# Logits summed by heads in all row blocks but the last, early loads for the last convolution, and a new written order

## The chip, the cores and the metric

The kernel runs on one core of one Trainium2 chip. The metric is the time of one execution on the device in microseconds (us). Of the kernel before there are three timed runs: 394.6, 395.1 and 396.57 us, median 395.1. The core has five engines with a queue each: TensorE (PE in the profile; its weight loads are PEld), VectorE (DVE), ScalarE (ACT), GpSimd (POOL) and SyncE (SP), which here issues nearly all DMAs. An engine takes its instructions strictly in the order of its queue.

## The reference

Four layers on x of 2048 rows and 512 columns in bfloat16: attention, convolution, attention, convolution, each on the layer-normalized x and added to x. The weights of the two attentions are the same, and those of the two convolutions too.

```python
def _A_ref(x, wqkv, wo):                      # 32 heads of 16, window 8, dilation 2
    qkv = (x @ wqkv).reshape(B, S, 3, H, Dh).transpose(2, 0, 3, 1, 4)
    q, k, v = qkv[0], qkv[1], qkv[2]
    idx = pos[:, None] - arange(8)[None, :] * 2   # masked where negative
    logits = einsum("bhsd,bhswd->bhsw", q, k[idx]) * Dh ** -0.5
    o = einsum("bhsw,bhswd->bhsd", softmax(logits), v[idx])
    return o.transpose(0, 2, 1, 3).reshape(B, S, D) @ wo

def _B_ref(u, A, B, C, log_dt, Dskip):        # a long convolution per column
    P = exp((exp(log_dt) * A)[:, :, None] * arange(L))
    K = einsum("dn,dnl,dn->dl", C, P, exp(log_dt) * B).real
    y = irfft(rfft(u, 2 * L) * rfft(K, 2 * L))[:L]
    return y + u * Dskip

x = x + _A_ref(layernorm(x)); x = x + _B_ref(layernorm(x))
x = x + _A_ref(layernorm(x)); x = x + _B_ref(layernorm(x))
```

## The kernel before

**Stages.** Six stages follow each other. Generation (`k_gen`, 0 to 107.9 us of the profile) builds the convolution kernel K from powers of the complex exponentials, and beside it normalizes x, turns it, makes the keys and queries of the first attention and its first three products. First attention (`LayerA.core` with CORE0, to 185.1). First convolution (`FftB.run` with ORDER0, to about 236.6), which also transforms K. The front of the second attention (ORDERF, to about 262): the end of the first convolution, normalization, transposes, keys. Second attention (`core` with CORE1, to 347.7). Second convolution (ORDER1, to 389.1), after which the last stores land.

**The order is written out by hand.** In a region of `tc.manual_schedule(engines=...)` each named engine issues its instructions as they are emitted. The strings ORDERK, CORE0, ORDER0, ORDERF, CORE1 and ORDER1 give the order of emission, one letter or word a step. Before, each stage has a region of its own, and where the instructions of one region fall among those of the next or among what stands between regions (loads, pools) is the scheduler's affair. The tile framework adds the waits between engines.

**An attention.** Rows lie as position p*16 + a, so a row block a of 128 rows holds every sixteenth; four of them are one block q (q = 0 to 3). The queries, keys and values of a block are projections on TensorE (`qproj1` L219, `front_k` L277, `v_proj` L395), each four matmuls into PSUM and a copy out by ScalarE (or DVE). The letters in the two CORE strings:

- m: a product of a block's queries with the eight shifted keys of one quarter ft of the columns (DVE, L342), into one of two buffers `prod`; l: its sum over the columns of a head on TensorE into the block's logits L (L350 or L354); x: their maximum (DVE, L414); e, r, n: exponentials and normalization (TensorE and ScalarE, L430 to L453).
- A block with q < NCOL sums by heads: eight matmuls with the 32 head indicators as weights stream the products, and the logits stand with the heads on the partitions; they are turned after the softmax (T, `turn` L455: eight transposes and a ScalarE copy). Another block sums by rows: 32 matmuls with the products as weights and eight columns of indicators. Before, NCOL is (2, 2).
- P: the products of one row block's attention with its eight shifted values (DVE, L472); S or V: their sum and transposition on TensorE by 64-row halves (S, L497) or whole (V, L487), with a ScalarE copy; O: the output projection, with the statistics for the next normalization; a and f: the normalization of one row block on DVE or ScalarE (L197, L195); b, d, t: its statistics.
- After the eighth and the sixteenth value projection SP copies rows of v_ext into its first part (L403, L404); the products P of even and of odd row blocks need the first and the second of these copies.
- Other letters are events of the stage: in CORE0 the tables of the inverse transform (c, 2 to 5), loads of K (1, 6), its rearrangement into k_perm (A to H, by the engine in KROWS), and w, the load of the matrix w2 in 32 DMAs (L596). In CORE1 the events 0 to 3 are what the front leaves over: keys of block 3 (P3), queries (Q0), and copies of shifted keys (x, e; `front_ext`).

**A convolution.** K and U (first transform step of K and of u), k and u (second step, with w2), m (the product of both spectra, DVE, L857), y or Y (first inverse step), and z, w, v (second inverse step, added to x). The letter A or D behind a step names the engine that copies the result out of PSUM. u goes through three buffers `ub`. In the first convolution the spectrum of K is stored to DRAM (`kf_dram`); the second reads it back into a ring of seven slots and three spare ones, three DMAs a slot (`kf_load`, L847, L849). The ring and the table g2 are allocated and asked for when the second convolution is opened (`open_mid`, L768), which the scheduler may place among the earlier stages' DMAs.

In generation the letters are: s, i, b (squares, products and copies of powers), M (one table of powers, DVE), T, U (the levels of another, DVE), p (their product on TensorE) and x (copied out), y and z (normalization, by the engines in ENGK), X (the first attention's first three products) and Z (their sums).

```python
    with tc.manual_schedule(engines=MAN_ALL):
        C = k_gen(...)
```

## Time and profile before

| what | value |
| --- | --- |
| median of three runs | 395.1 us (394.6 to 396.57) |
| profiled execution: span, its own time | 393.9 us |
| VectorE busy | 372.8 us, 95% |
| ScalarE busy | 331.1 us, 84% |
| TensorE busy | 324.1 us, 82% |
| GpSimd busy | 65.5 us, 17% |
| TensorE clock granted | 0.999 |
| DMA traffic | 54.18 MB |

The profile is of one execution; the page gives its span, from the first to the last instruction, as the only time of that execution. In a table by stage, a row has the stretch in us, its length, then busy time and number of instructions for each engine, the granted clock, the mean busy share of the 16 DMA engines and GB/s. In a list in order of time a row has start, length, engine, line of the kernel, operation, the tile written and those read, their shapes, how many instructions are merged in the row, and, in brackets, how long the engine idled before it and what ended that. Neighbouring instructions of one engine can overlap by some 0.1 us, so the distance of two starts is a better price than a length. In the groups, behind the shape and the number of instructions stand their busy time in us, the mean length in ns, and the idle time before them.

### The profile page before, as it was taken

The page shows a single profiled execution, that of the slowest core. Times are in us where ns is not written, and L with a number is a line of the kernel's source. Part 1 is how long each engine was busy: PE and PEld are TensorE (multiplying, and loading weights), DVE is VectorE, ACT ScalarE, POOL GpSimd, SP SyncE. Part 2 cuts the span into 40 slices and gives each one's busy share as a digit, 9 for nine tenths or more (in the row PEclk, how much of TensorE's full clock was granted, in tenths as well). Part 3 has the DMA queues.
Part 4 walks back from the last instruction along what each step waited for, and adds up shares of the span by engine and source line. Part 5 has one row for each costly group of instructions (what it writes and reads, how often), then busy time and mean ns, then how long its engine had stood idle before and what let it go on. Part 6 is the DMA issues. An engine that isn't in the chain of part 4 may idle for free.

```text
span 393.9 us, 14769 instructions
## 1 busy us (share of the span) xinstructions
PE 324.1 (82%) x6451; PEld 231.5 (59%) x6499; DVE 372.8 (95%) x449; ACT 331.1 (84%) x568; POOL 65.5 (17%) x97
## 2 busy tenths in 40 slices
PE   3000258999999999999998899999999999998894
PEld 2000116756734676766887888543456676677894
DVE  6999999999989999999999989979999999989984
ACT  7999999997558799899999998574666779889992
POOL 9402960000280000010731201100000020000000
PEclk9999999999999999999999999999999999999999
DMA  7953810414027556277678634820253057604525
GB/s 209 396 155 50 83 53 3 106 28 108 9 66 198 128 168 176 61 228 235 215 265 300 216 110 110 300 62 2 73 141 96 3 170 222 195 13 155 171 68 152
DMA packets 68303, 54.18 MB, mean 138 GB/s; under 512 B 33545, under 2 KB 58670, under 8 KB 67982
## 3 DMA queue, kind: packets, MB, share of 16 engines
q1 hardware_dynamic: 66566, 48.70, 42.7%
q0 software_dynamic: 1664, 4.52, 3.1%
q8 instruction: 51, 0.84, 0.9%
q14 instruction: 14, 0.11, 0.1%
q10 hardware_dynamic: 8, 0.00, 0.0%
HBM read 30.15 MB, written 13.24 MB: 110 GB/s over the span
## 4 chain that ended last, share of the span: by engine, by line
PE 49%; DVE 21%; ACT 19%; issue 5%; DMA 2%; SPq 2%; POOL 1%; DVEq 0%; ACTq 0%; POOLq 0%
PE pq L398 7%; PE po L497 5%; PE pq L508 4%; PE pq L223 4%; PE pk L1277 3%; DVE A_t L1119 3%; ACT ub L869 3%; DVE B_t L1119 3%; PE L L354 3%; PE pp L282 3%; ACT a1s L800 3%; PE pp L1215 2%; DVE t L857 2%; SPq L596 2%; PE L L350 2%
## 5 line engine op out<-in xcount | busy, mean ns | idle before, releaser
L472 DVE TENSOR_TENSOR pav<-attn,v_ext 128x4096 bf16<-128x4096 bf16 (+1 forms) x34 | 72.3, 2160 | 0.3 <-DMA v_ext<-v_ext 0.3
L342 DVE TENSOR_TENSOR prod<-qT,kT_ext 128x4096 bf16<-128x4096 bf16 x29 | 65.6, 2288 | 3.0 <-PE L L350 2.1
L1119 DVE TENSOR_TENSOR A_t<-A_t,pow_t 128x1024 bf16<-128x1024 bf16 (+4 forms) x46 | 38.2, 873 | 0.2
L1205 PE MATMUL pt<-ident,x_blk 128*128 128x128 bf16 x64 | 6.0, 241 | 39.4 <-ACT x_blk L195 39.4
L508 PE MATMUL pq<-wop,oT 128*128 128x512 bf16 x121 | 31.5, 379 | 2.4 <-issue 1.9
L497 PEld LDWEIGHTS <-pav 64*128 64x128 bf16 x1728 | 26.9, 95 | 9.9 <-DVE pav L472 3.3
L869 ACT CAST ub<-pb 128x1024 bf16<-128x1024 f32 x32 | 32.6, 1110 | 0.0
L1215 PE MATMUL pp<-xnT,kT_ext 128*128 128x512 bf16 x88 | 25.5, 413 | 7.3 <-ACT xnT L1208 4.3
L818 PE MATMUL pb<-a1s,w_sb 128*128 128x64 bf16 x768 | 27.4, 193 | 3.8 <-ACT ub L869 1.4
L398 PE MATMUL pq<-wv,xnT 128*128 128x512 bf16 x123 | 30.0, 379 | 0.5 <-ACT kgs L1285 0.3
L497 PE MATMUL po<-ident,pav 64*128 64x64 bf16 x1728 | 29.9, 190 | 0.6 <-ACT oT L499 0.2
L400 ACT CAST v_ext<-pq 128x512 bf16<-128x512 f32 x32 | 18.7, 586 | 13.5 <-PE pq L398 11.1
L800 ACT CAST a1s<-pb 128x1024 bf16<-128x1024 f32 x29 | 28.5, 1063 | 1.2 <-PE pb L811 1.2
L1205 PEld LDWEIGHTS <-x_blk 128*128 128x128 bf16 x64 | 4.6, 107 | 41.3 <-ACT x_blk L195 40.2
L818 PEld LDWEIGHTS <-w_sb 128*128 128x128 bf16 x768 | 25.1, 98 | 6.0 <-issue 4.0
L178 POOL TENSOR_TENSOR ln_rstd<-ln_rstd,ln_mh 128x4 f32<-128x4 f32 x2 | 4.0, 1995 | 120.1 <-DVE ln_rstd L177 66.9
L1277 PEld LDWEIGHTS <-A_t 128*64 128x64 bf16 (+1 forms) x512 | 21.7, 103 | 3.8 <-DVE A_t L1119 0.2
L800 DVE CAST a1s<-pb 128x1024 bf16<-128x1024 f32 x19 | 22.5, 1220 | 1.4 <-PE pb L811 1.0
L1277 PE MATMUL pk<-B_t,A_t 128*64 128x84 bf16 (+1 forms) x512 | 23.5, 201 | 0.2
L223 PE MATMUL pq<-xnT,kT_ext 128*128 128x512 bf16 x85 | 22.6, 379 | 0.9 <-issue 0.5
L225 ACT CAST qT<-pq 128x512 bf16<-128x512 f32 x24 | 14.0, 585 | 9.8 <-PE pq L223 9.5
L398 PEld LDWEIGHTS <-xnT 128*128 128x128 bf16 x128 | 11.9, 97 | 15.3 <-issue 2.4
(264 smaller groups left out, 919.9 us busy)
## 6 DMA issues: line engine op xcount, KB each, us to landing
w_sb<-w_dram SPq DMA_DIRECT2D x64, 128.0 KB, 3.0
w_dram<-xnT SPq DMA_DIRECT2D x1, 4096.0 KB
kf_ring<-kf_dram SPq DMA_DIRECT2D x13, 256.0 KB, 3.8
kf_ring<-kf_dram SPq DMA_DIRECT2D x26, 128.0 KB, 3.6
v_ext<-v_ext SPq DMA_DIRECT2D x4, 784.0 KB, 6.1
x_blk<-in_A_x_dram SPq DMA_DIRECT2D x4, 512.0 KB, 4.7
kT_ext<-in_A_wqkv_dram SPq DMA_DIRECT2D x4, 512.0 KB, 9.2
x_sb<-in_A_x_dram SPq DMA_DIRECT2D x4, 512.0 KB, 6.3
```

The lines of the kernel that those rows point to most:

```text
L223: nc.tensor.matmul(pq[:], lhsT=self.wqk[:, dt, ft * P:(ft + 1) * P], rhs=self.xnT[:, dt, q * 512:(q + 1) * 512], start=(dt == 0), stop=(dt ...
L342: nc.vector.tensor_tensor(pr, self.qT[q][:, ft].unsqueeze(1).to_broadcast([P, W, 4, P]), kap, ALU.mult)
L398: nc.tensor.matmul(pp[:], lhsT=xnT[:, dt, a * P:(a + 1) * P], rhs=wv[:, dt, :], start=(dt == 0), stop=(dt == NDT - 1))
L472: nc.vector.tensor_tensor(pv[:, i], attn[:, n % 4].unsqueeze(2).to_broadcast([P, W, DH // parts, H]), vap, ALU.mult)
L497: nc.tensor.matmul(po[:, h, 0, i * nt + ft, :], lhsT=pvf[rows, i, w, ft * P:(ft + 1) * P], rhs=ident[rows, rows], start=(w == 0 and ft + i ...
L508: nc.tensor.matmul(pw[:], lhsT=oT[:, ftp, :], rhs=self.wo[:, ftp, :], start=False, stop=(ftp == NDT - 1))
L800: (self.nc.scalar.copy if eng == "act" else self.nc.vector.tensor_copy)(dst, src)
L818: nc.tensor.matmul(p2[:, j, :], lhsT=self.w2[:, ec * EC + j, :], rhs=a1s[:, ec * EC + j, :], start=True, stop=True)
L869: nc.scalar.copy(ub[:], p2)
L1119: return lambda: nc.vector.tensor_tensor(*args)
L1215: nc.tensor.matmul(pps[kind, b, ft][:], lhsT=la.wqk[:, dt, c:c + P], rhs=la.xnT[:, dt, b * 512:(b + 1) * 512], start=(dt == 0), stop=(dt = ...
L1277: nc.tensor.matmul(o, lhsT=lhs, rhs=Bt[:, ri, c * CH + ql].rearrange("p b g -> p (b g)"), start=(not half and j % 4 == 0 and ri == 0), sto ...
```

## The change

- NCOL becomes (4, 3): all four blocks of the first attention and the first three of the second sum their logits by heads; block 3 of the second stays by rows.
- The whole program is one region in which DVE, ScalarE, TensorE and SP issue in the order of emission; GpSimd is ordered in generation alone, as before.
- In the second attention g2 and the seven ring slots get tiles of their own on the other side of the memory, allocated before `core`, and are asked for by the events 0 to 3 of CORE1, behind the front's remaining steps; the convolution starts with these seven slots filled and asks for three more. In the first convolution g2 is asked for by the word g of ORDER0.
- The w2 load is cut into four parts (W) of eight DMAs.
- The front's thirteen remaining steps become events of their own (RKEYS), each with its engine (RROWS).
- All six order strings are others. In ENGK two normalizations (y, z) go from DVE to ScalarE; in KROWS two parts of k_perm go from ScalarE to DVE.

```diff
-sbiCCiCisCGiCbiMsaibsCbMiibMcMsTibMGicGMMbasMGiGibTMTMbsGGTabbiTTiaTsicGTbbacTiTibcGsTMTGiaGaMlM
...
-kUTzkzUkTxkTKttkKkUkUkpKekekxKUUpkkKqxpKUqUUxUkUoEUUkpQkUKkpxUUoxpUXpxXKopxxZXZZ
+iCsCaibCiCbMsiGMisbisCMiibbCMsaiibcMTMMbcisGibbscbGMTibTiTsMbTbTciibTMasTaGcTGaGMaGaiiMMTGGGMlaG
...
+kkkKkTkUlkKzUzTUTqzUzpUpUUUtKxpeUtUqUExUQepkkUUxxkUKUpEpokxXkUKkoKkkxpKpZXoXxXZZ
 """
 ORDER0 = """
-KD KA KA KA KA KD KD KA KA KD kA KD KA KD KA kA kD UA KD UA UD UA UA UD UA UD
-kA KD kA kD u kD u m u kA kD UA UA m u kD UA kD m UA UA u m kD UA m
-u u UD UA m u kA u m m kA kD kA m yD u m u YA m u YA yD u u m
-m YA u m u m w000A m YA yA YD YA yA yD yA w010D yA
+g KD KA KA KA KA KD KD KA KA KD KA kD KA KD KA KD kA UA UD KA UD kA UD UA kD UA UD UA kA kD u kD u m
+m u u kA kD u kD UA UA m UA m u UD u kD UA UA m m m u UA kA kD UA kA m kD kA u yD u u m YD u m m m
+YA yA u u u m u YA w000A YA m m m yD YA YA yA yD yA w010D yA
 """
 ORDERF = """
-yD h00 h01 yA YA v101A v100A v110A v111A h10 z12A a0 p0 v113A h11 a1 p1 z02A S z03A n0D T0 n1G E00D
-v103D E01A P03 H2 a2 T1 P01 E10D p2 E11D Q00 n2G H3 P00 a3 P02 P11 P12 p3 T2 E21D E20D P10 P13
-P22 P20 n3D T3 E31A P23 P21 E30D x1
+yD h01 yA YA v100A v101A h00 v110A v111A h10 a0 v103D p0 n0D v113A h11 z03A S a1 z12A T0 E01D E00A
+p1 z02A n1G P02 H2 Q00 P01 T1 a2 E10A p2 P03 E11D P10 P00 n2G H3 P12 a3 T2 E20A p3 P13 E21D n3D P23
+P11 P21 T3 E30D P20 E31D x1D P22
 """
 ORDER1 = """
...
-YA m m m w001A w000D yA yA w011D YA w010D yA yD yA yD yA v102D v101A v112D v111A v113D v103D v100A v110D
...
+v112D v110D v113D v103D v101A v111A
 """
 CORE0 = """
-vmvvvvqlvmxvlmemvvrclvnlmqTlqmxmvvelvvvvcmlqcPlSPrqOmncml1VTxPPqeSmr2lqP4OlSOSm5PqOP3S7lmOSnlPOx
-VPeOPSPrOSnPO6SObbP9SwOP8SPdBHOVaOPfSEdObatSaCaAfataGDFO
+mmvvvvlcvvmvllxemvmqrlmcnvlcxqTqvlcvvmmevvvvPqlr1qlPmnql4VTmmqO3lxSPq62lOS57mPlePSmOrSlPnOSPO8xT
+SPbeOSrOPSnOPSTOPP9SbdOSPfdOPSOSaaPPfOFSfAOSfabWWWWODtGtCEHfB
 """
 CORE1 = """
-0m1l2ml3mqvvmvllqvmqvxqelmlvmmvvqrlnqlmTvmxPPvlvvqvvqvmlmvqlqelmSrqnxmPSPqTOSOSlePOlPmrSOSnmOOPl
-bSlPSPwOxdfPVaePOSraPOnVabPOSPdOSOPSbPOSfaOftSdafaaftO
+DACBFGEJIvHmKmllLN0123qmvqvmlvqmllvvmxvvqlqmemlqrlmnvqTvxmevllvPqvvvmvmqPlrlnmxqqTmSleqSmlPrOSOP
+PmSnOSPPTOlblSOSPOxSedPOOrPSbnSPfdPOSWWWWfPOSOPSfPOSafOSbPdOafaStatafOf
 """
-NCOL = (2, 2)
-ENGK = dict(b="AAAAAAAAAAAAAAAAA", y="AAAAAAAAAADA", z="DAAA", e="AAAAAAAA", K="AAAAAAAAAAAAAAAA", Q="AAAAAAAA", x="AAAAAAAAAAAAAAAA")
+NCOL = (4, 3)
+ENGK = dict(b="AAAAAAAAAAAAAAAAA", y="AAAAAAAAAAAA", z="AAAA", e="AAAAAAAA", K="AAAAAAAAAAAAAAAA", Q="AAAAAAAA", x="AAAAAAAAAAAAAAAA")
 STATD = (3,)
-KROWS = "DADAADDD"
+RKEYS = "ABCDEFGHIJKLN"
+RROWS = "AADDAADAAADDA"
+KROWS = "DDDDDADD"
...
+    def load_w2(self, w2_dram, part):
+        if part == 0:
+            w2 = self.keep.tile([P, NDT * (2 * D + (NA + 14) * P)], BF16, name="w2_sb", tag="slot")
...
+        for c in range(8 * part, 8 * part + 8):
             self.nc.sync.dma_start(self.w2[:, c * 4:(c + 1) * 4, :], w2_dram[:, c * 4:(c + 1) * 4, :])
...
+def kf_read(nc, kc, kf_dram, n):
+    g, ec = divmod(n, NEC)
+    nc.sync.dma_start(kc[0::2], kf_dram[g, ec])
+    for r in range(2):
+        nc.sync.dma_start(kc[1::2, r], kf_dram[g, ec, :, 1 - r])
...
     def open_mid(self):
         tc, nc, t = self.tc, self.nc, self.tag
-        nc.sync.dma_start(self.g2[:], self.g2_dram[:])
         if t:
-            for n in (4, 3):
-                kr = self.c_mid.enter_context(tc.tile_pool(name=f"b{t}_kf{n}", bufs=1, reuse_waits="tile"))
-                kr = kr.tile([P, n, 2, DQG, EC], BF16, name=f"kf_ring{n}")
-                self.ring += [kr[:, i] for i in range(n)]
+            self.nkf = len(self.ring)
+            self.kf = dict(enumerate(self.ring))
             self.ring += self.extra
...
     nc = tc.nc
+    ctx.enter_context(tc.manual_schedule(engines=MAN))
...
-    with tc.manual_schedule(engines=MAN_ALL):
+    with tc.manual_schedule(engines={ET.Pool}):
         C = k_gen(tc, nc, lambda sp: build_a_consts(nc, cpool, sp, consts), ins, kd, la, x_v, lnst,
...
-        ev = {"w": lambda: la.load_w2(w2_dram),
-              "0": last(("P", 3, 0), ("P", 3, 1), ("x", 0), ("x", 2), ("P", 3, 2), ("Q", 0, 1), ("e", 0), ("Q", 0, 2)),
-              "1": last(("P", 3, 3), ("Q", 0, 3)), "2": last(("e", 1), ("e", 2)), "3": last(("e", 3))}
...
+    ring_ctx = ExitStack()
+    g2p = ring_ctx.enter_context(tc.tile_pool(name="b1_g2", bufs=1, side="right", reuse_waits="tile"))
+    g2 = g2p.tile([P, 2, 16, P], BF16, name="g2_sb")
+    ring = []
+    for n in (4, 3):
+        kr = ring_ctx.enter_context(tc.tile_pool(name=f"b1_kf{n}", bufs=1, side="right", reuse_waits="tile"))
...
+    ev = la.w2_loads(w2_dram)
+    ev |= {"0": lambda: nc.sync.dma_start(g2[:], g2_dram[:]), "1": lambda: ring_loads(0, 1), "2": lambda: ring_loads(2, 3),
+           "3": lambda: ring_loads(4, 5, 6)}
+    rest = (("P", 3, 0), ("P", 3, 1), ("x", 0), ("x", 2), ("P", 3, 2), ("Q", 0, 1), ("e", 0), ("Q", 0, 2),
+            ("P", 3, 3), ("Q", 0, 3), ("e", 1), ("e", 2), ("e", 3))
+    for c, e, (op, *ix) in zip(RKEYS, RROWS, rest):
+        ev[c] = lambda e=e, op=op, ix=ix: front[op](*ix, dict(A="act", D="dve")[e])
```

130 lines of the change are left out of this document (64 added, 66 removed).

## The prediction

> **What bounds the kernel now.** I read the page's busy shares first, then a table of busy time by stage, then the instructions in order of time at the joins of the stages, and last the groups by shape, for prices.
>
> ```profile
> span 393.9 us, 14769 instructions
> PE 324.1 (82%) x6451; PEld 231.5 (59%) x6499; DVE 372.8 (95%) x449; ACT 331.1 (84%) x568; POOL 65.5 (17%) x97
> ```
> ```profile
> core 0: us, PE busy (x) PEld busy (x) DVE busy (x) ACT busy (x) POOL busy (x), PEclk, DMA share, GB/s
> 0.00:107.90 107.90, 56.93 (x702) 38.68 (x712) 103.64 (x168) 96.33 (x178) 33.73 (x49) 1.00 0.43 109
> 107.90:185.10 77.20, 74.69 (x1496) 46.82 (x1513) 75.19 (x61) 66.00 (x129) 10.27 (x19) 1.00 0.55 155
> 185.10:236.60 51.50, 46.92 (x1440) 43.65 (x1435) 49.89 (x52) 51.13 (x58) 15.03 (x25) 1.00 0.63 222
> 236.60:262.00 25.40, 24.77 (x231) 16.98 (x231) 22.45 (x69) 18.34 (x35) 3.50 (x4) 1.00 0.59 183
> 262.00:347.70 85.70, 83.18 (x1552) 49.98 (x1569) 83.75 (x70) 62.28 (x130) 2.94 (x1) 1.00 0.36 105
> 347.70:389.10 41.40, 37.59 (x1045) 35.37 (x1044) 37.91 (x36) 37.04 (x42) 0.00 (x0) 1.00 0.39 117
> ```
>
> The stages are: kernel generation, first attention, first convolution, the front of the second attention, second attention, second convolution. VectorE (DVE) idles 21.1 us in all, and 4.3 of that lies in generation and 4.8 behind the last instruction. In both attentions DVE (75.19 of 77.20, 83.75 of 85.70) and TensorE (74.69, 83.18) are both nearly full; the first convolution is bound by ScalarE (51.13 of 51.50); the front by TensorE (24.77 of 25.40). So DVE work that is removed counts in the first, second and fifth stage alone, TensorE work in the fifth, and ScalarE work only where it delays the third.
>
> **The engine sums.** Shape by shape:
>
> ```profile
> L197 DVE TENSOR_SCALAR xnT<-x_sb,ln_rstd,ln_nb 128x512 bf16<-128x512 bf16 x16 | 6.3, 415 | 0.1
> L195 ACT ACTIVATE xnT<-x_sb,ln_nb,ln_rstd 128x512 bf16<-128x512 bf16 x8 | 6.4, 814 | 0.0
> L1459 DVE COPY k_perm<-k_rl 128x1024 bf16<-128x1024 bf16 x5 | 2.0, 421 | 0.0
> L1459 ACT COPY k_perm<-k_rl 128x1024 bf16<-128x1024 bf16 x3 | 3.1, 1044 | 0.2 <-DMA w_sb<-w_dram 0.2
> L273 DVE COPY xnT<-pt 128x1024 bf16<-128x1024 bf16 x6 | 3.9, 678 | 1.2 <-PE pt L271 1.2
> L295 DVE COPY kT_ext<-kT_ext 128x508 bf16<-128x508 bf16 x5 | 1.4, 290 | 0.2 <-ACT kT_ext L285 0.2
> L461 ACT COPY attn<-L 128x1024 bf16<-128x1024 bf16 x4 | 4.1, 1017 | 0.5 <-PE L L459 0.5
> L800 DVE CAST a1s<-pb 128x1024 bf16<-128x1024 f32 x19 | 22.5, 1220 | 1.4 <-PE pb L811 1.0
> ```
>
> DVE: two normalizations of generation go to ScalarE (y and z of ENGK), -2 x 0.415 = -0.83. In CORE0 three more do ("a" 6 to 3, "f" 2 to 5), -1.25, and two parts of k_perm come back (KROWS), +0.84. In ORDER0 K has two DVE evacuations fewer, k one and U one more: 4 x 1.22, sum 0. In ORDERF one E goes to ScalarE, -0.68, in a stage that TensorE bounds, so it is worth nothing. In the second attention one kT copy (-0.29) and two normalizations (-0.83) go. On DVE's path that is -0.83 - 0.41 - 1.12 = -2.4; six small instructions that run on the heels of others cost some 0.08 less than their duration, so I take **-2.0** (bounds -1.5 and -2.4).
>
> ScalarE takes what DVE gives (7 x 0.814, less 2 x 1.044, and about 1.6 for the E and the kT copy) and three copies of turned attention, 3 x 1.017: some 8 us. In the attentions its cover is 11.2 us of idle time in the first (77.20 - 66.00) and 23.4 in the second. If that cover were gone, in the first it would delay the ScalarE-bound convolution: see rival C.
>
> TensorE: prices by starts of neighbours, 119.01 to 119.56 (0.55) for a sum by heads, 126.63 to 127.44 (0.81) by rows, 118.47 to 119.01 (0.54) for eight 128-column matmuls, which is also what turning a block takes. The two last rows are from the chain of waits.
>
> ```profile
> 118.47 0.61 PE L441 MATMUL pq<-ex,ident 128*128 128x128 bf16 x8
> 119.01 0.61 PE L350 MATMUL L<-prod,ind 128*32 128x512 bf16 x8
> 119.56 0.39 PE L398 MATMUL pq<-wv,xnT 128*128 128x512 bf16 x1
> 126.63 0.94 PE L354 MATMUL L<-ind,prod 128*128 128x8 bf16 x32
> 127.44 3.61 PE L398 MATMUL pq<-wv,xnT 128*128 128x512 bf16 x15
> 138.48 1.89 PE po L487 x32
> 153.30 1.11 PE po L497 x64
> ```
>
> Blocks 2 and 3 of the first layer and 2 of the second change form: 12 sums, -12 x 0.26 = -3.1, and three turns, +1.6. Four rows of the attention output that were summed whole (V, 1.8) are summed by halves (S, 1.1): -2.8. In all -4.3, of which 4 x 0.26 - 0.54 + 2 x 0.7 = 1.9 lies in the second attention. The mask matmuls (0.2) stay. [...]
>
> **The joins.** The first attention starts late:
>
> ```profile
> 101.31 6.69 DVE L342 TENSOR_TENSOR A_pr<-qT,kT_ext 128x4096 bf16<-128x4096 bf16 x3
> 107.91 0.29 DVE L295 COPY kT_ext<-kT_ext 128x508 bf16<-128x508 bf16 x1
> 109.78 4.50 DVE L342 TENSOR_TENSOR prod<-qT,kT_ext 128x4096 bf16<-128x4096 bf16 x2 [1.57 <-PE L L350]
> ```
>
> Its first product waits 1.57 us until the third of generation's products is summed, because TensorE has value projections in between. With one region for the program TensorE keeps the written order, the sums (Z Z) first and "mm vvvv" after them: the third sum follows its product by 0.55, less the 0.29 copy that runs meanwhile, plus a hand-over of 0.1. The wait becomes 0.4: **-1.2** (bounds 0 and -1.57). TensorE then starts its projections 1.3 us later; the order has room for that: by adding up each queue from the start of the stage (0.86 a projection, 0.55 or 0.81 a sum, 2.2 a product), the last sum of block 2 has 26.9 us of TensorE work up to its end and DVE asks for it after 28.7 us of its own work, where before the pair is 29.4 against 28.7. The closest pair is the second sum of block 2, 23.2 against 24.3.
>
> The front: TensorE does as many projections behind the last transposes as before.
>
> ```profile
> 257.35 1.06 PE L271 MATMUL pt<-ident,xn 128*128 128x128 bf16 x16
> 258.24 4.26 PE L282 MATMUL pp<-xnT,kT_ext 128*128 128x512 bf16 x19
> 261.98 2.29 DVE L342 TENSOR_TENSOR prod<-qT,kT_ext 128x4096 bf16<-128x4096 bf16 x1
> ```
>
> Two projections of block 2 and one of block 3 (0.86 each), an evacuation and a copy come before the first product in both orders, so 3.74 us behind the transposes: 0. In the second attention DVE now idles 1.95. In the new order the third product must wait for the first sum, which has eight projections ahead of it: 258.24 + 10 x 0.86 + 0.55 = 267.4 against 261.98 + 2 x 2.2 + 0.4 = 266.8, a wait of 0.6. The next pairs come out within 0.2 of each other (the sum of product (0,3) ends 14.2 us of TensorE work after 259.97, at 274.2; product (1,1), which needs its buffer, is due at 267.4 + 3 x 2.2 = 274.0), and in the second half TensorE is ahead by 2, having 1.9 us less. I leave 1.25 of the 1.95: **-0.7** (bounds -1.4 and +0.7).
>
> Generation's order: DVE asks for the ninth power (for product step 17) 31.7 us into its own work, and ScalarE has it after 33.4; the largest such lead before was 1.3 us and made no wait. **+0.4** (bounds 0 and +1). First convolution: equal sums, ScalarE full, so nothing to gain; products now come two and three together with three ub buffers, **0** (bounds -0.3 and +1.5). Second convolution: as many instructions on each engine as before, **0** (bounds -0.5 and +0.5).
>
> The DMAs: by its name the change asks for the ring early. Before, SP does so already:
>
> ```profile
> 246.13 0.51 SPq L847 DMA_DIRECT2D kf_ring<-kf_dram  x1
> 246.69 1.24 SPq L849 DMA_DIRECT2D kf_ring<-kf_dram  x2
> 255.75 0.59 SPq L849 DMA_DIRECT2D kf_ring<-kf_dram  x1
> 281.46 0.67 SPq L403 DMA_DIRECT2D v_ext<-v_ext  x1
> 283.18 2.04 SPq L849 DMA_DIRECT2D kf_ring<-kf_dram  x1
> v_ext<-v_ext SPq DMA_DIRECT2D x4, 784.0 KB, 6.1
> ```
>
> Five ring slots are asked for from 246 on and the rest from 283, and the second convolution shows no wait for them: so this part does little here, 0. The w2 loads in four parts and the g2 load stay in SP's order.
>
> Sum: -2.0 - 1.2 - 0.7 + 0.4 = -3.5 on the profiled 393.9, which lies 1.2 below the median of the three runs (395.1): taken off that, **391.6**. The runs differ by 2 us, so 0.5% (2.0 us) is about what can be told from no change.
>
> **The rivals.** B, the waits go too: with TensorE relieved, all of DVE's idle time in the front and the second attention (2.95 + 1.95, of which 0.7 is counted) but some 1 us vanishes: 391.6 - 3.2 = 388.4. For it: TensorE is what these waits name (L271, L350). Against: the front keeps its TensorE work.
>
> C, handed back: ScalarE's added work in the first attention (3 x 0.81 - 2 x 1.04 + 2 x 1.02 = 2.4) arrives at the convolution that it bounds, and all gained before it (0.8 + 0.4 + 1.2 - 0.4 = 2.0) is lost: 393.6. Against: ScalarE idles 11 us there, though most of it before 130.
>
> D, slower: SP's queue in the second attention. The written order puts g2 and seven ring slots (22 DMAs, 1.9 us a slot by the rows from 246.13 on, 13.7 in all) ahead of the copies of v_ext, for which the first output product waits. Their room is that of the front's xn, last read by the transposes at 258.24; SP is then at v_ext by 272, and the copies have 1.6 to issue and 6.1 to land. The product comes near 287, so the ring must begin by 266. If its room is only free with something later, every us beyond 266 is a us: held until 272.5, the time is 391.6 + 6.5 = 398.1.
>
> [...]
>
> **How the numbers follow.** Forecast 0.45 (its own range 390 to 393), B 0.15, C 0.2, D 0.15, E 0.05. Faster by over 0.5% (under 393.1): forecast and B, 0.6; within: C and E, 0.25; slower (over 397.1): D, 0.15. The range goes from B (388.4 less 0.4 for the runs' lower spread, 388.0) to a D that is 3 us late with the upper spread of 1.5, 396.2.
>
> **What would show it.** Right: the first product of the first attention follows the last of generation with under 0.7 us of idle; DVE near 370 busy; the first convolution starts near 182.5 and takes as long as now; the second attention shortens by 1.5 to 2. Wrong: a DVE wait for v_ext's DMA near 287 (D), a ScalarE that enters the first convolution behind DVE (C), waits for ub in it, or generation ending after 108.

## The result and the profile after

The changed kernel takes 390.43 us (median, 390.08 to 391.12), the kernel before 395.34 in runs beside it: ratio 0.9868 with a 95% interval of [0.9844, 0.9893], 4.9 us faster, by the interval 1.1 to 1.6%. The profiled execution took 390.13, its span is 388.4, 5.5 under the span of before. From the page: the span, the busy shares, and, from its part on the DMA queues, the queue that brings instructions (packets, MB, share of the engines).

```profile
span 388.4 us, 14497 instructions
...
PE 319.6 (82%) x6312; PEld 219.9 (57%) x6361; DVE 369.8 (95%) x442; ACT 336.1 (87%) x578; POOL 68.2 (18%) x97
...
q8 instruction: 49, 0.80, 0.8%
```

The table of busy time by stage:

```profile
core 0: us, PE busy (x) PEld busy (x) DVE busy (x) ACT busy (x) POOL busy (x), PEclk, DMA share, GB/s
0.00:106.45 106.45, 56.29 (x706) 37.84 (x714) 102.49 (x167) 97.45 (x180) 33.73 (x49) 1.00 0.43 111
106.45:181.98 75.53, 72.69 (x1375) 40.27 (x1395) 74.67 (x60) 67.01 (x132) 12.95 (x19) 1.00 0.54 156
181.98:233.55 51.57, 47.38 (x1444) 43.96 (x1439) 49.82 (x51) 51.34 (x58) 15.04 (x25) 1.00 0.64 224
233.55:258.36 24.81, 24.70 (x232) 16.98 (x232) 21.91 (x68) 18.98 (x36) 3.50 (x4) 1.00 0.26 80
258.36:343.68 85.32, 81.48 (x1525) 45.69 (x1543) 83.20 (x67) 64.37 (x134) 2.94 (x1) 1.00 0.44 137
343.68:384.14 40.46, 36.90 (x1044) 35.18 (x1044) 37.74 (x35) 36.26 (x40) 0.00 (x0) 1.00 0.37 113
```

DVE is busy 3.0 us less than before, TensorE 4.5 less, ScalarE 5.0 more. Every stage but the first convolution (51.57 for 51.50) became shorter. Instructions in order of time, at the joins and at the places where DVE still waits:

```profile
107.24 4.50 DVE L342 TENSOR_TENSOR prod<-qT,kT_ext 128x4096 bf16<-128x4096 bf16 x2 [0.51 <-PE L L350]
...
181.98 1.22 DVE L810 CAST a1s<-pb 128x1024 bf16<-128x1024 f32 x1
...
182.31 3.76 ACT L810 CAST a1s<-pb 128x1024 bf16<-128x1024 f32 x4
...
255.24 0.51 SPq L756 DMA_DIRECT2D kf_ring<-kf_dram  x1
...
264.00 9.21 DVE L342 TENSOR_TENSOR prod<-qT,kT_ext 128x4096 bf16<-128x4096 bf16 x4 [0.55 <-ACT qT L225]
...
275.70 0.67 SPq L403 DMA_DIRECT2D v_ext<-v_ext  x1
...
299.15 2.29 DVE L342 TENSOR_TENSOR prod<-qT,kT_ext 128x4096 bf16<-128x4096 bf16 x1 [0.28 <-issue]
...
342.19 0.16 DVE L185 SCALAR_TENSOR_TENSOR ln_nb<-ln_ag,ln_rstd 128x3 f32<-128x3 f32 x1 [0.53 <-ACT ln_rstd L156]
```

The first attention's first product waits 0.51 and not 1.57. ScalarE enters the first convolution together with DVE (182.31 and 181.98). The ring is asked for from 255.24 on, and the copies of v_ext follow at 275.70 without a DVE wait behind them. In the second attention DVE waits 0.55, 0.28 and 0.53, 1.36 in all; before, such waits of over 0.2 us came to 1.43:

```profile
271.76 2.29 DVE L342 TENSOR_TENSOR prod<-qT,kT_ext 128x4096 bf16<-128x4096 bf16 x1 [0.27 <-ACT v_ext L400]
...
277.79 4.50 DVE L342 TENSOR_TENSOR prod<-qT,kT_ext 128x4096 bf16<-128x4096 bf16 x2 [0.41 <-ACT qT L225]
...
282.78 4.49 DVE L342 TENSOR_TENSOR prod<-qT,kT_ext 128x4096 bf16<-128x4096 bf16 x2 [0.49 <-PE L L350]
...
303.23 4.49 DVE L472 TENSOR_TENSOR pav<-attn,v_ext 128x4096 bf16<-128x4096 bf16 x2 [0.26 <-DMA v_ext<-v_ext]
```

So that stage kept its waits. All of DVE's idle time in it, by the tables of busy time, went from 1.95 (85.70 less 83.75) to 2.12 (85.32 less 83.20). DVE's waits in the second convolution, of before and then of the changed kernel (us in total, times, longest):

```profile
DVE x_sb L935 <- PE pb L933: 2.3, 5, 0.8
DVE a1s L800 <- PE pb L811: 1.0, 2, 0.8
```
```profile
DVE x_sb L943 <- PE pb L941: 1.6, 3, 0.8
DVE a1s L810 <- PE pb L821: 0.8, 1, 0.8
```

They fall from 3.3 to 2.4, which is what that stage became shorter.

### The profile page after: what moved, and what is told of

Its sections match the earlier page's. It is cut to its first block, busy times and chain, and to the rows that moved or that the text cites. A ratio compares the mean times of both kernels' runs of the same rounds, so it can differ in the third digit from the quotient of the medians.

```text
span 388.4 us, 14497 instructions
## 1 busy us (share of the span) xinstructions
PE 319.6 (82%) x6312; PEld 219.9 (57%) x6361; DVE 369.8 (95%) x442; ACT 336.1 (87%) x578; POOL 68.2 (18%) x97
## 4 chain that ended last, share of the span: by engine, by line
PE 41%; ACT 17%; DVE 8%; issue 5%; DMA 1%; DVEq 0%; ACTq 0%
PE pq L398 7%; PE pq L223 5%; DVE pav L472 4%; PE pp L282 4%; ACT a1s L810 3%; ACT ub L877 3%; PE po L497 3%; PE L L350 3%; PE pq L508 2%; PE pb L891 2%; PE pb L821 2%; PE pb L895 2%; PE pb L940 2%; PE L L424 2%; PE pb L941 1%
## 5 line engine op out<-in xcount | busy, mean ns | idle before, releaser
L497 PEld LDWEIGHTS <-pav 64*128 64x128 bf16 x1984 | 30.8, 95 | 11.7 <-DVE pav L472 4.3
L497 PE MATMUL po<-ident,pav 64*128 64x64 bf16 x1984 | 34.3, 190 | 0.2
L877 ACT CAST ub<-pb 128x1024 bf16<-128x1024 f32 x32 | 31.7, 1116 | 0.0
L810 ACT CAST a1s<-pb 128x1024 bf16<-128x1024 f32 x30 | 29.4, 1054 | 1.4 <-PE pb L821 1.3
L178 POOL TENSOR_TENSOR ln_rstd<-ln_rstd,ln_mh 128x4 f32<-128x4 f32 x2 | 6.0, 2984 | 108.7 <-DVE ln_rstd L177 66.1
L223 PE MATMUL pq<-xnT,kT_ext 128*128 128x512 bf16 x89 | 23.7, 380 | 0.3
L810 DVE CAST a1s<-pb 128x1024 bf16<-128x1024 f32 x18 | 21.4, 1216 | 1.3 <-PE pb L821 1.0
L508 PEld LDWEIGHTS <-oT 128*128 128x128 bf16 x128 | 12.5, 98 | 12.4
```

What stands on the lines that cost most here:

```text
L223: nc.tensor.matmul(pq[:], lhsT=self.wqk[:, dt, ft * P:(ft + 1) * P], rhs=self.xnT[:, dt, q * 512:(q + 1) * 512], start=(dt == 0), stop=(dt ...
L497: nc.tensor.matmul(po[:, h, 0, i * nt + ft, :], lhsT=pvf[rows, i, w, ft * P:(ft + 1) * P], rhs=ident[rows, rows], start=(w == 0 and ft + i ...
L508: nc.tensor.matmul(pw[:], lhsT=oT[:, ftp, :], rhs=self.wo[:, ftp, :], start=False, stop=(ftp == NDT - 1))
L810: (self.nc.scalar.copy if eng == "act" else self.nc.vector.tensor_copy)(dst, src)
L877: nc.scalar.copy(ub[:], p2)
```

## The experiments

All times below by one ruler, read from DVE's instructions in order of time: generation ends with its third product; the join ends with the first product of the first attention; a convolution begins with DVE's first evacuation (line 810), the front with its first statistics, the second attention with its first product; the second convolution ends with DVE's last instruction. Medians and ratios are those of the timed runs, each ratio against the kernel before in the same series. The kernel before had medians of 395.34 to 395.73 in these series, so a difference of some 0.4 us between medians of different series says nothing. Where TensorE does not pause (below), the same work takes the same time within some 0.03 us from profile to profile; the generation of rows_shift, 0.24 over that of the changed kernel, is an exception that stays open.

| kernel | median us | ratio, 95% interval | gen. | join | 1st att. | 1st conv. | front | 2nd att. | 2nd conv. |
| --- | --- | --- | --- | --- | --- | --- | --- | --- | --- |
| before | 395.34 | 1 | 108.00 | 1.78 | 75.31 | 51.47 | 25.42 | 86.58 | 40.54 |
| changed | 390.43 | 0.9868 [0.9844, 0.9893] | 106.52 | 0.72 | 74.74 | 51.57 | 24.81 | 86.13 | 39.65 |
| join_alone | 396.10 | 1.0006 [0.9980, 1.0032] | 108.05 | 0.72 | 77.07 | 52.82 | 25.40 | 86.67 | 40.54 |
| region_alone | 396.44 | 1.0008 [0.9985, 1.0032] | 108.06 | 0.72 | 77.24 | 51.53 | 25.40 | 86.56 | 40.55 |
| rows_again | 394.81 | 0.9981 [0.9963, 0.9999] | 106.50 | 0.72 | 75.44 | 52.99 | 25.79 | 87.18 | 39.63 |
| rows_shift | 394.05 | 0.9951 [0.9925, 0.9977] | 106.76 | 0.71 | 75.46 | 51.57 | 24.81 | 87.17 | 41.26 |
| after_shift | 392.49 | 0.9918 [0.9894, 0.9942] | 106.53 | 0.71 | 74.73 | 53.38 | 24.91 | 87.25 | 40.71 |
| shift_256 | 391.23 | 0.9895 [0.9849, 0.9941] | 106.52 | 0.71 | 75.12 | 51.69 | 24.81 | 86.11 | 39.65 |
| ring_late | 392.33 | 0.9904 [0.9881, 0.9927] | 106.51 | 0.72 | 74.73 | 51.58 | 24.80 | 87.41 | 39.90 |
| heads_all | 393.08 | 0.9927 [0.9903, 0.9952] | 106.53 | 0.72 | 74.74 | 51.58 | 25.35 | 88.56 | 40.11 |
| old_generation | 393.32 | 0.9947 [0.9918, 0.9976] | 108.38 | 0.72 | 74.75 | 52.61 | 25.00 | 86.35 | 39.64 |
| old_engines | 395.28 | 0.9996 [0.9968, 1.0024] | 107.28 | 0.72 | 75.29 | 54.37 | 24.88 | 86.98 | 39.64 |
| old_ends | 391.96 | 0.9907 [0.9874, 0.9940] | 106.52 | 0.71 | 74.73 | 51.59 | 25.52 | 86.47 | 40.54 |
| queries_first | 391.75 | 0.9895 [0.9850, 0.9940] | 106.51 | 0.72 | 75.29 | 51.93 | 25.14 | 86.11 | 39.64 |

### The join alone, and the region alone

In the kernel before, generation and the first attention in one region:

```diff
-    with tc.manual_schedule(engines=MAN_ALL):
+    reg = ExitStack()
+    reg.enter_context(tc.manual_schedule(engines=MAN))
+    with tc.manual_schedule(engines={ET.Pool}):
         C = k_gen(...)
...
-    with tc.tile_pool(name="ctmp_g2", bufs=1) as g2tmp, tc.manual_schedule(engines=MAN):
+    with tc.tile_pool(name="ctmp_g2", bufs=1) as g2tmp:
...
         late = la.core(x_sb, u, lnp, CORE0, ev, 3)
+    reg.close()
```

> The kernel before with one change: generation and the first attention are one region, so TensorE sums generation's third product before it begins the value projections. By the theory of the join, the idle time of VectorE before the first product of the first attention falls from 1.57 us to about 0.5, the first convolution starts 1.1 us earlier (184.0 for 185.1) and the time is 1.1 us under the kernel before, about 394.2. By the rival (TensorE's projections start 1.1 us later and some later product or sum is late by as much) the first product starts early too, but a new wait of about 1 us stands later in the first attention, the first convolution starts at 185.1 and the time is that of the kernel before, 395.3.

And the changed kernel with everything of before but the region, the split w2 load and the ring's place (all six strings, NCOL, ENGK, KROWS and the front's engines as before; w becomes WWWW, the front's rest and the ring's loads stand where the events 0 to 3 stood):

> The changed kernel with the order strings, the engines and the counts of sums by heads of the kernel before: what is left of the change is the one region, the w2 load in four parts and the ring on the other side of the memory, asked for behind the front's last step. If the region is worth the join alone: 1.1 us under the kernel before, 394.2, and every other stage as long as before (front 25.4, second attention 85.7, second convolution 41.4). If it is the region that shortens the front and the second convolution too (the changed kernel's are 0.6 and 0.9 us shorter), about 392.7. If the old orders need what the scheduler did between the regions, it is slower than 395.3, by waits at the stages' joins.

Neither is faster than before. The wait at the join falls to 0.51 in both, as the theory has it, but the rival comes with it; DVE in order of time in the kernel with the join alone:

```profile
108.77 4.49 DVE L342 TENSOR_TENSOR prod<-qT,kT_ext 128x4096 bf16<-128x4096 bf16 x2 [0.51 <-PE L L350]
114.74 1.23 DVE L414 TENSOR_REDUCE mx<-L 128x128 bf16<-128x1024 f32 x1 [1.48 <-PE L L325]
```

TensorE starts its projections later, and the maximum of the first block waits 1.48 for that block's logits. The first attention with its join is 0.7 longer than before (77.79 for 77.09; region alone 77.96). The changed kernel has the same join and none of this wait: the order written for it (CORE0 begins with the products and not with a projection) keeps the 1.06. That is by elimination: in the changed kernel the engines, ORDERK and the form of the sums are each undone below, and none of them brings a wait of that size back; CORE0 was not undone alone. In region_alone the front, the second attention and the second convolution are as before to 0.02, so the region does nothing for them.

### The form of the sums, and an unexpected guest

The changed kernel with two blocks by heads, and the T's of the others dropped from the strings:

```diff
-NCOL = (4, 3)
+NCOL = (2, 2)
```

> The changed kernel with only the first two blocks of each attention summed by heads, as before; the three turns that go with the others are dropped. TensorE's work grows by 12 x 0.26 - 3 x 0.54 = 1.5 us, 0.5 of it in the second attention, ScalarE's falls by 3 x 1.02. By the theory that VectorE's path carries the gain, the time grows by 0.3 us (0 to 0.7), to about 390.7, all of it in the second attention. By the rival that the sum by heads carries the gain, it grows by 2 us or more, with waits for the sums in both attentions. [...]

The time rises by over 4 us, far more than the theory. But the stages do not agree with the rival either: the first convolution, which has no such sum, grows by 1.42 and the front by 0.98. TensorE in order of time shows two pauses there, each in the middle of a series of matmuls, and "issue" says that nothing in the profile ended them:

```profile
192.49 0.31 PE L828 MATMUL pb<-a1s,w_sb 128*128 128x64 bf16 x5 [0.86 <-issue]
...
235.24 0.19 PE L895 MATMUL pb<-WpJ,t 64*128 64x64 bf16 x1 [0.81 <-issue]
```

Each matmul has a weight load ahead of it, so the n-th weight load is row 2n - 1 of TensorE's instructions. Counted so, the two pauses stand at rows 5049 and 7353, 2304 = 9 x 256 apart. So the same kernel was run with 128 instructions more, in time in which TensorE idles:

```diff
             pt = xps[b, d] = la.ps_tr.tile([P, 2, 4, P], BF16, name="pt")
+            for _ in range(64 if b + d == 0 else 0):
+                nc.tensor.transpose(pt[:, 0, 0, :], ident[:], ident[:])
```

> The changed kernel with two blocks of each attention by heads (as in rows_again), and in TensorE's idle time before 44 us 64 more transposes, each with its weight load, that nothing reads: 128 instructions. In rows_again two pauses of TensorE that nothing in the trace explains (0.86 us at 192.49, 0.81 at 235.24) stand 2304 = 9 x 256 instructions apart. By the theory that TensorE's program comes in pieces of 256 instructions (the instruction queue moves 52 pieces of 16 KB) and a piece is late where other DMAs crowd it, the pieces now begin 128 instructions earlier in the work: the two pauses are gone from their places, any new one lies a multiple of 256 instructions from where they were in TensorE's list (128 earlier or later in the work), and the first convolution falls from 52.99 us towards the changed kernel's 51.57. By the rival that the pauses belong to that work, they recur there and the convolution stays at 53.0. By a second rival, the added work itself shows: generation would be longer than 106.5.

Both pauses are gone, and the first convolution and the front are those of the changed kernel to 0.00 (51.57, 24.81). A new pause of 1.50 stands at 383.33, row 13231. What remains is the price of the form itself: the first attention 0.72 longer (75.46 for 74.74) and the second 1.04 (87.17 for 86.13). DVE's waits in the second attention of that kernel, beside a fourth of 0.54 at its end:

```profile
264.95 9.20 DVE L342 TENSOR_TENSOR prod<-qT,kT_ext 128x4096 bf16<-128x4096 bf16 x4 [0.54 <-ACT qT L225]
290.31 2.29 DVE L342 TENSOR_TENSOR prod<-qT,kT_ext 128x4096 bf16<-128x4096 bf16 x1 [0.52 <-ACT qT L225]
301.13 2.29 DVE L342 TENSOR_TENSOR prod<-qT,kT_ext 128x4096 bf16<-128x4096 bf16 x1 [0.43 <-PE L L354]
```

They are 2.03 in all, 0.67 more than with the sums by heads. TensorE's busy time in the second attention is 0.57 more in rows_again than in the changed kernel (82.05 for 81.48), which is the difference of the prices of the two forms less a turn (0.5), so no further price of either form shows.

### The pauses: two shifts of the changed kernel

The same 64 unread transposes in the changed kernel, and then 128 of them.

> The changed kernel with the same 64 unread transposes before 44 us. The work on every engine's path is the same, so a difference from the changed kernel's 390.4 can only be where the program's pieces now begin. By the theory of late pieces: pauses of 0.6 to 1.3 us appear in the middle of TensorE's work where the DMAs are dense (the first convolution, or from 345 us on), 0 to 2.5 us in all, 390.4 to 392.9, and every stage without one is as long as before the shift to within 0.05 us. By the rival that nothing hangs on it: 390.4 within 0.4, all stages as long as before.

> The changed kernel with 128 unread transposes in TensorE's idle time before 44 us, 256 instructions, twice those of the shift by 128. By the theory of pieces of 256 instructions, every piece begins at the same place in the work as in the changed kernel: the time goes back from 392.5 to about 390.4 (within 0.6), and what pauses there are lie at the same places in the work as the changed kernel's piece borders, not at those of the shift by 128 (233.8, 332.2, 384.5). By the rival that the added instructions themselves do the harm (more pieces to bring, or a later start of generation's work), it is slower than the shift by 128, 392.5 to 394.6.

With 128 instructions more the profile has five new pauses of over 0.5 us and its stages are 4.1 us longer in all, the median 2.1; with 256 more, work that is twice as much, the median is 391.23, 0.8 over the changed kernel where at most 0.6 was expected, and the stages are 0.5 longer. The profiled execution of after_shift, 394.23, is the longest of its seven and that of shift_256, 390.58, the shortest of its four, and the intervals of the two ratios overlap; so it is the places of the pauses that tell, more than the times. Matmuls of the second pause of after_shift:

```profile
233.82 0.20 PE L895 MATMUL pb<-Wp,t 64*128 64x64 bf16 x2 [0.81 <-issue]
```

The pauses of at least 0.5 us in mid-series in all profiles, from the list of TensorE or of its weight loads; the row is that of the weight load behind the pause:

| kernel | at us | us | row | row mod 256 |
| --- | --- | --- | --- | --- |
| queries_first | 145.78 | 0.79 | 2233 | 185 |
| old_engines | 192.40 | 0.80 | 4537 | 185 |
| after_shift, old_generation | 190.82, 195.19 | 0.55, 0.67 | 4793 | 185 |
| rows_again | 192.49 | 0.86 | 5049 | 185 |
| join_alone | 197.15, 202.25 | 0.60, 0.66 | 5047, 5303 | 183 |
| after_shift, heads_all | 233.82, 234.37 | 0.81, 0.50 | 7097 | 185 |
| rows_again | 235.24 | 0.81 | 7353 | 185 |
| after_shift | 327.62, 332.18 | 0.73, 0.58 | 9903, 10159 | 175 |
| ring_late, heads_all | 337.01, 341.35 | 1.13, 1.80 | 10415 | 175 |
| ring_late | 355.31 | 1.07 | 11183 | 175 |
| heads_all | 385.33 | 0.58 | 12463 | 175 |
| after_shift | 384.49 | 0.95 | 12719 | 175 |
| rows_shift | 383.33 | 1.50 | 13231 | 175 |

(Idle times named "issue" that stand at the same work in every kernel, such as 1.23 at 149.32 ahead of line 441, are not counted: they are waits that the profile does not resolve.) Whatever work lies there, the row has one remainder by 256 in a stretch of the program: 185 up to row 7353 and 175 from 9903 on, and 183 in join_alone, which is made from the kernel before; why it changes on the way is open. The 0.5 us of shift_256 fit too: most of it is a pause of 0.44 at 169.60, row 3769, remainder 185. So TensorE's program comes in pieces of 256 instructions, and a pause stands where a piece begins. The page's instruction queue moved 49 pieces of 16 KB (0.80 MB) for the changed kernel's 12,722 rows (6,361 weight loads with a matmul each), and 52 for the 13,254 of rows_again, some 256 rows a piece. Most borders show nothing (of the some 50 of after_shift five have a pause in the table), and single ones cost 0.5 to 1.8 us.

The traces hold the packets of that queue one by one, and they tell what TensorE waits for. Every pause in the table, and the one at 169.60, ends 1.3 to 1.6 us after a packet has landed, and that packet had started only 1.1 to 3.8 us after TensorE began the piece before. In after_shift, for instance, TensorE begins a piece at 230.10, the packet runs from 231.17 to 232.37, and the pause ends at 233.83. So the next piece is brought while one runs, and TensorE pauses when start, transfer (0.9 to 2.1) and the 1.3 to 1.6 behind it take longer than the work of 256 instructions, which in dense stretches is some 3 to 5 us.

Not every execution has the same pauses: queries_first has the program of the changed kernel up to 258 us and pauses at 145.78, where the changed kernel's profile shows nothing. There are two ways into a pause. Two of those near 234 stand where hardly any DMA moves (share 0.02 and 0.03 from 231 to 236 us), behind packets that started 1.07 after the border, where 1.0 is the median in the changed kernel: TensorE, at some 80 instructions a us, was through with the piece sooner. Most of the others stand behind packets that started 2 to 3.8 us after it; what held those up is open. Neither before nor the changed kernel shows a pause in its profile.

### The ring's loads late

```diff
-DACBFGEJIvHmKmllLN0123qmvqvmlvqmllvvmxvvqlqmemlqrlmnvqTvxmevllvPqvvvmvmqPlrlnmxqqTmSleqSmlPrOSOP
-PmSnOSPPTOlblSOSPOxSedPOOrPSbnSPfdPOSWWWWfPOSOPSfPOSafOSbPdOafaStatafOf
+DACBFGEJIvHmKmllLNqmvqvmlvqmllvvmxvvqlqmemlqrlmnvqTvxmevllvPqvvvmvmqPlrlnmxqqTmSleqSmlPrOSOP
+PmSnOSPPTOlblSOSPOxSedPOOrPSbnSPfdPOSWWWW0123fPOSOPSfPOSafOSbPdOafaStatafOf
```

> The changed kernel with g2 and the ring's seven slots asked for behind the w2 load, in SP's order behind both copies of v_ext: from about 312 us on and not from 254.8. By the theory that the early request is worth nothing, the time is that of the changed kernel, 390.4 (within 0.4), and the second convolution is 40.5 us long as with the early loads. By the rival that the early loads are what made the second convolution shorter, it is 41.4 again and the time about 391.3; products of the second convolution would wait for the ring's DMAs.

No stage waits for the ring, but the median is 1.9 us over the changed kernel's: neither theory. The 22 loads now run from 329.3 on, in a row with those of w2. TensorE in order of time, and its stretch from 334 to 337.5 by the table of busy time, in this kernel and then in the changed one (the last two numbers are DMA share and GB/s):

```profile
337.01 0.52 PE L497 MATMUL po<-ident,pav 64*128 64x64 bf16 x23 [1.13 <-issue]
...
334.00:337.50 3.50, 2.23 (x68) 1.42 (x71) 3.22 (x6) 2.23 (x5) 0.00 (x0) 1.00 0.99 379
```
```profile
334.00:337.50 3.50, 3.19 (x84) 1.89 (x87) 3.40 (x8) 3.19 (x9) 0.00 (x0) 1.00 0.79 225
```

TensorE's list is the same, row by row; with the DMAs at 0.99 it pauses 1.13 us at row 10415, and DVE waits 1.21 instead of nothing for what follows. The packet of that piece started 3.1 us after the piece before began, in the changed kernel 0.6. That the loads held it up would fit, but it is not shown: heads_all, whose loads are early, pauses at the same row 10415, and for longer. The four timed runs (391.62 to 392.77) are all above the changed kernel's, while the intervals of the two ratios overlap.

### All blocks by heads

```diff
-PmSnOSPPTOlblSOSPOxSedPOOrPSbnSPfdPOSWWWWfPOSOPSfPOSafOSbPdOafaStatafOf
+PmSnOSPPTOlblSOSPOxSedPOOrPSbnSPfdTPOSWWWWfPOSOPSfPOSafOSbPdOafaStatafOf
...
-NCOL = (4, 3)
+NCOL = (4, 4)
```

> The changed kernel with the last block of the second attention summed by heads too, and turned two steps behind its normalization. TensorE has 4 x 0.26 - 0.54 = 0.5 us less, ScalarE one copy of 1.02 more, in the last third of the second attention. By the theory that the form is worth what TensorE saves on the second attention's path, that stage falls by 0.3 to 0.5 us and the time to about 390.0. By the rival that the turn comes too late for the block's first output product (VectorE waits for the turned copy), the stage grows by 0.5 to 1.5 us.

2.6 us slower. The front and the second convolution are longer by the pauses at 234.37 and 385.33, and of the second attention's 2.43 the pause at 341.35 is most; DVE does not wait for the turned copy, so the rival is wrong, and the theory's gain does not appear either. The rest, some 0.6, lies in small waits (0.23 for an output sum, 0.19 and 0.16) and is otherwise unexplained.

### The orders of generation, front and second convolution

ORDERK of before in the changed kernel:

> The changed kernel with generation's order of before (ORDERK), the two normalizations still on ScalarE. By the prediction's step the new order costs 0.4 us, so generation's third product would end at 106.1 and the time fall by 0.4 to 390.0. By the rival that the order itself carries part of the 1.5 us which generation became shorter (0.83 of it is the two normalizations), it ends at 107.1 and the time rises by 0.6 to 391.0, with the idle time of VectorE in generation back by as much.

Generation ends at 108.38, 1.86 later: the opposite of the prediction's step, and beyond the rival. With the old order the two normalizations on ScalarE make DVE wait:

```profile
80.62 0.49 DVE L1127 TENSOR_TENSOR A_t<-A_t,pow_t 128x256 bf16<-128x256 bf16 x2 [0.34 <-ACT A_t L1244]
...
106.09 2.29 DVE L342 TENSOR_TENSOR A_pr<-qT,kT_ext 128x4096 bf16<-128x4096 bf16 x1 [0.30 <-ACT kT_ext L295]
```

DVE is busy 103.43 for 102.56 although the lengths of its instructions sum to the same, some 114.5 us: in the new order more of them follow each other without a gap and overlap.

ORDERF and ORDER1 of before (with x1D for x1):

> The changed kernel with the old order of the front (ORDERF, its last copy on VectorE as before) and of the second convolution (ORDER1). The prediction gave both orders nothing; the changed kernel's front is 0.6 us shorter than that of before and its second convolution 0.9. If the orders are what did it, the front is 25.4 us again and the second convolution 40.5, and the time grows by 1.5 to about 391.9. If it is the ring's early loads, the form of the sums or another thing, the front stays at 24.8 and the second convolution at 39.7, and the time at 390.4.

The front is 25.52, the second convolution 40.54, as before, with the waits of before in it:

```profile
DVE x_sb L943 <- PE pb L941: 2.3, 5, 0.8
DVE a1s L810 <- PE pb L821: 1.0, 2, 0.8
```

So the two orders are worth 0.71 and 0.89, and 0.34 in the second attention.

### The engines

```diff
-SPbeOSrOPSnOPSTOPP9SbdOSPfdOPSOSaaPPfOFSfAOSfabWWWWODtGtCEHfB
+SPbeOSrOPSnOPSTOPP9SbdOSPadOPSOSfaPPaOFSaAOSfabWWWWODtGtCEHaB
...
-PmSnOSPPTOlblSOSPOxSedPOOrPSbnSPfdPOSWWWWfPOSOPSfPOSafOSbPdOafaStatafOf
+PmSnOSPPTOlblSOSPOxSedPOOrPSbnSPfdPOSWWWWaPOSOPSaPOSafOSbPdOafaStftaaOf
...
-ENGK = dict(b="AAAAAAAAAAAAAAAAA", y="AAAAAAAAAAAA", z="AAAA", e="AAAAAAAA", K="AAAAAAAAAAAAAAAA", Q="AAAAAAAA", x="AAAAAAAAAAAAAAAA")
+ENGK = dict(b="AAAAAAAAAAAAAAAAA", y="AAAAAAAAAADA", z="DAAA", e="AAAAAAAA", K="AAAAAAAAAAAAAAAA", Q="AAAAAAAA", x="AAAAAAAAAAAAAAAA")
...
-KROWS = "DDDDDADD"
+KROWS = "DADAADDD"
```

> The changed kernel with the engines of before for the normalizations (two of generation, three of the first attention, two of the second back on VectorE) and for k_perm (two parts back on ScalarE); every order stays. By the prediction's term of VectorE's work, generation grows by 0.83 us (its third product ends at 107.3), the first attention by 3 x 0.415 - 2 x 0.42 = 0.41, the second by 0.83, and the time by 2.0 to about 392.4; ScalarE falls by 7 x 0.81 - 2 x 1.04 = 3.6. By the rival that these stages have slack enough on VectorE in the new order, they stay within 0.2 us of the changed kernel's. Single pauses of TensorE at multiples of 256 instructions come on top, in any stage from 180 us on.

Generation grows by 0.76, the first attention by 0.55, the second by 0.85: 2.16, where 2.07 was expected. Not expected was the first convolution, 2.80 longer. ScalarE in order of time:

```profile
182.11 2.94 ACT L1468 COPY k_perm<-k_rl 128x1024 bf16<-128x1024 bf16 x3
184.96 0.57 ACT L512 CAST x_sb<-pq 128x512 bf16<-128x512 f32 x1
185.43 1.01 ACT L810 CAST a1s<-pb 128x1024 bf16<-128x1024 f32 x1
```

Three parts of k_perm stand in its queue at the join, and it enters the convolution that it bounds 2.14 behind DVE (183.29), where in the changed kernel it is 0.33: 1.81 of the 2.80. A ScalarE wait of 1.02, behind the pause at 192.40, is the rest.

### A projection moved

```diff
-DACBFGEJIvHmKmllLN0123qmvqvmlvqmllvvmxvvqlqmemlqrlmnvqTvxmevllvPqvvvmvmqPlrlnmxqqTmSleqSmlPrOSOP
+DACBFGEJIHvmKmllLN0123qmvqvmlvqmllvvmxvvqlqmemlqrlmnvqTvxmevllvPqvvvmvmqPlrlnmxqqTmSleqSmlPrOSOP
```

> The changed kernel with one projection of values moved behind the last of the remaining query projections at the start of the second attention. In the changed kernel the third product there waits 0.55 us for its queries. If nothing else is late, that wait goes and the second attention falls by 0.5 us (86.13 to 85.6), the time to about 389.9, which would be the best of all. If the values' projection or the sums behind it become late by as much, the wait stands at a later product and the stage stays at 86.1.

```profile
265.23 4.49 DVE L342 TENSOR_TENSOR prod<-qT,kT_ext 128x4096 bf16<-128x4096 bf16 x2 [0.54 <-ACT v_ext L400]
```

The third product waits as long as before (0.54 for 0.55), now put down to another ScalarE copy. So it does not wait for its queries, as the row of the changed kernel says, but for something that the swap leaves alone; the first sum, with the same projections ahead of it and the buffer that the product needs, fits. In old_generation and old_engines, where the same product waits longer, the row names that sum:

```profile
267.46 4.49 DVE L342 TENSOR_TENSOR prod<-qT,kT_ext 128x4096 bf16<-128x4096 bf16 x2 [0.90 <-PE L L350]
```

This one is of old_generation. The other stages are longer by pauses (0.79 at 145.78). No kernel beats the changed one.

## Why the prediction was right or wrong

The time was forecast at 391.6 and came out at 390.4. The sum was -3.5 and the spans differ by -5.5, of which 0.54 lies behind DVE's last instruction (4.80 to 4.26; that rest was 3.1 to 5.5 in the other profiles, so it tells nothing). By stages, forecast and then measured: generation -0.43 and -1.48, the join -1.2 and -1.06, the first attention -0.41 and -0.57, the first convolution 0 and +0.10, the front 0 and -0.61, the second attention -1.82 and -0.45, the second convolution 0 and -0.89. (The forecasts sum to 0.4 more than -3.5, which the sum takes off for small instructions.) So the good number is in part luck: the 1.4 by which the second attention fell short came, and more, from generation's order, the front and the second convolution, which were booked as a cost or at nothing.

- **DVE's work, -2.0: right as a price in the new order,** where it costs 2.16 to move it back in the three stages named. Against before it shows in full in generation and the first attention, but in the second DVE's busy time fell only 0.55 (83.75 to 83.20) where 1.12 were forecast: the lengths of its instructions sum to 1.23 less (88.59 and 87.36), but what they overlap each other shrank too. ScalarE's busy time grew by 5.0, not by some 8; TensorE's fell by 4.5, where 4.3 were forecast.
- **The join, -1.2: right in place and size (-1.06; the wait became 0.51 where 0.4 was forecast), with too little said of the condition.** The sums of queues that gave it "room" were made for the new order and hold there; in the old order the same join is eaten by a wait of 1.48.
- **The sums by heads in the first attention, nothing: wrong, -0.72.** The step gave TensorE's savings to the second attention alone, because in the first the queues came out within a margin of about 1 us. They were too close for that: there the rows' form brings waits of 0.30 and 0.23.
- **The second attention's waits, -0.7: right against the wrong ruler.** Between the two forms in the new order the waits differ by 0.67. But the new order has waits of its own (0.55 at the third product, foreseen as 0.6, and 0.53 at the end), and against before there was nothing left: 1.43 to 1.36 for the waits, and 1.95 to 2.12 for all of DVE's idle time, of which the step left 1.25. The stage fell by 0.45, where 1.5 to 2 stood in what would show it right.
- **Generation's order, +0.4: wrong in sign.** DVE does not wait for the ninth power; the new order is worth 1.86 once the normalizations are on ScalarE, and 0.72 with them where they were (old_engines 107.28, before 108.00). The step looked for one late operand and did not ask what the moved work does to the old order.
- **The front, 0: wrong, -0.61.** The step counted the projections behind the last transposes, and TensorE lost its time earlier: 25.42 with 24.77 busy became 24.81 with 24.70.
- **The second convolution, 0: wrong, -0.89.** "As many instructions on each engine as before" says nothing of waits, and DVE's waits for TensorE were 3.3 us of that stage.
- **The first convolution, 0: right (+0.1),** but by an edit that was booked as a cost: in the new order, where k_perm's parts stand at the end of the attention, k_perm moved to DVE lets ScalarE enter in time. Rival C's mechanism is real; old_engines shows it, with 1.81.
- **Rival D: did not happen.** The ring is asked for from 255.24, ahead of the 266 named, and its loads are out of SP's way by 268.8. The early loads gain nothing against before, which asked early too; asked for behind w2 the median was 1.9 higher, but the profile shows pauses there and no wait for the ring. **Rival E,** given 0.05, was a price of a sum by heads on TensorE beyond its 0.55: the busy times leave no room for one (0.57 between the two forms in the second attention, where their prices give 0.5). **Rival B** named the front's waits, which fell a little, and those of the second attention, which stayed.

The single terms, each undone in the changed kernel, add up to more than the whole gain, since each order string was written for the rest of the change; they are prices of the last step, not shares.

## What to carry to other kernels

Price a change of the written order by the waits of the new order, queue by queue and in all its stages, and not by the waits that the old profile shows: equal counts of instructions hide waits that a reordering can take away, and a wait taken away alone can come back two steps later. In a kernel that hangs on single microseconds, compare stages and not spans: on this chip TensorE paused for 0.5 to 1.8 us at single borders of 256 instructions, waiting for the next piece of its program, so an edit that only shifts its program can look 2 us better or worse.

## What the runs showed of the hardware

TensorE's pauses at program pieces were not expected; the table above has them. A second thing is how to read the granted clock. With 128 unread transposes between 7 and 16 us, the profile shows it at half from 20 to 54 us; in the changed kernel, whose TensorE also idles up to 44.38 (36.52 us long, 28.65 in shift_256), it shows the full clock throughout. Tenths of the span in 40 slices, of the kernel shift_256 and then of the changed one:

```profile
PE   6600188889999999999998899999999999987895
PEclk9955579999999999999999999999999999999999
```
```profile
PE   3000178889999998999998999999999998987895
PEclk9999999999999999999999999999999999999999
```

The matmuls themselves do not differ. In both kernels the first projections, of 512 columns each, start 0.427 us apart from 51.8 to 53.5 us and 0.215 apart from 54.8 on, the same to a few ns. The rows of the changed kernel:

```profile
51.41 3.17 PE L1223 MATMUL pp<-xnT,kT_ext 128*128 128x512 bf16 x7 [0.51 <-ACT xnT L1216]
54.80 1.46 PE L1223 MATMUL pp<-xnT,kT_ext 128*128 128x512 bf16 x6 [0.23 <-ACT kT_ext L1228]
```

So its TensorE came out of the pause at half speed too. Its trace has no entry of the clock before 54.43, and the profile shows such a stretch as full. The distances of the matmuls show half speed in both kernels, the clock row shows it in shift_256 alone. What halves the clock is not shown, nor what that costs: both kernels have it, and generation ends at 106.52 in both.
